# Transposing the attention output for the MLP: by DMA instead of TensorE and ScalarE

## The chip, the cores and the metric

The kernel runs on one core of a Trainium2 chip. The metric is the device time of one execution in microseconds. Engines are named as in the profile: PE (TensorE, with PEld for its weight loads), DVE (VectorE), ACT (ScalarE), POOL (GpSimd) and SP (SyncE, which here only issues DMAs).

## The reference

A linear attention (RWKV-5) over 4 batches, 8 heads, 768 tokens and a head dimension of 48, and then an MLP on its 3072 x 384 output. Cut to what is computed:

```python
state = np.zeros((B, H, D, D))
for t in range(S):
    cur = einsum('bhd,bhe->bhde', u[None] * k[:, :, t], v[:, :, t])
    y[:, :, t] = einsum('bhd,bhde->bhe', r[:, :, t], state + cur)
    state = w[None, :, :, None] * state + einsum('bhd,bhe->bhde', k[:, :, t], v[:, :, t])
x = y.transpose(0, 2, 1, 3).reshape(B * S, H * D)        # 3072 x 384
h = x @ w_in                                             # 384 x 2048
g = where(h >= 1, h, where(h <= -1, 0, (h + 1) ** 2 / 4))
out = g @ w_out                                          # 2048 x 384
```

## The kernel before

The tokens are cut into chunks of 128. A **unit** is one chunk of one batch (24 units), a **group** is the same chunk of two batches (12 groups of 2 units, 256 tokens). For each group the inputs R and K (float32, 384 KB each) are loaded by DMAs issued from SP (`load_rk`, lines 79 and 80), and V, cast to bf16, by DMAs from POOL (line 84). POOL also issues the loads of the MLP's weights: w_in in two halves before the loop, w_out in two halves at step 3. R and K have three buffers each.

One loop over steps `t` (line 379) carries all stages, each with its own offset; four steps belong to a group. All instructions are issued in the order in which the program writes them (`manual_schedule`), so each engine, SP among them, has one fixed queue. In a step the order is:

- `att0` on even steps (transposes of R and K on PE, copied to SBUF by DVE as TT), `att1` on odd steps (A on PE, masked by DVE into AT), from step 4g for group g
- at t = 4m, for m from 1: `load_rk` of group m + 2
- `act_end`: DVE forms `gt` from the square and h of the step before
- `mm1` (twelve matmuls `hp <- xT, w_in_sb`, line 310, four such parts to a group) and `act` (two ScalarE passes, lines 321 and 323). Group g begins `mm1` at t = 4g + 7
- `att2` on even steps (t = 4g + 2 and 4g + 4): the state update Sp, the attention output Y on PE, and DVE's sum `y` (line 271, bf16, two buffers); then `new_state`
- `att3` and `att4` on odd steps (t = 4g + 3 for the group's first unit, 4g + 5 for its second): the transposes of `y` (line 292) into the PSUM tile X, and the ScalarE copy (line 299) into one half of `xT[g]`. X takes the same PSUM buffer (tag `y`) as Y. Then `decay` on POOL
- `product` and `u_term`, the elementwise products, mostly on POOL, for groups ahead
- `mm2` (eight matmuls, line 341). On two steps of each group the result is copied by ScalarE (`o_sb`, line 347) and stored by a DMA from SP (line 349)

So `xT[g]` is what ties the attention to the MLP: both of its halves must be written before `mm1` of group g starts. The offset of the MLP is `L1`:

```python
L1, L2 = 7, 11
at_a, at_b, at_1, at_2, at_p = at(0), at(2), at(L1), at(L2), at(-4)
```

Before the loop, SP has issued R and K of groups 0, 1 and 2, and u.

Of the kernel before, what the change touches and what calls it, by code (L numbers as in the profile page):

```python
# [9 lines left out]
BF16 = mybir.dt.bfloat16  # L10
# [4 lines left out]
P = 128  # L15
# [3 lines left out]
UNITS = 2  # L19
# [3 lines left out]
def kernel(  # L23
# [11 lines left out]
    nc = tc.nc  # L35
# [6 lines left out]
    nK = DM // P  # L42
# [14 lines left out]
    ps1 = ctx.enter_context(tc.tile_pool(name="ps1", bufs=1, space=bass.MemoryType.PSUM))  # L57
# [8 lines left out]
    def load_tiles(g):  # L66
        R = loads.tile([P, UNITS * H, D], F32, name="R", tag="R")
        K = loads.tile([P, UNITS * H, D], F32, name="K", tag="K")
        V = loads.tile([P, UNITS * H, D], BF16, name="V", tag="V", bufs=5)
        loaded[g] = (R, K, V)  # L70
# [6 lines left out]
    def load_rk(g, j0=0, j1=UNITS):  # L77
        R, K, V = loaded[g]
        nc.sync.dma_start(out=R[:, j0 * H : j1 * H, :], in_=source(r, g, j0, j1))  # L79
        nc.sync.dma_start(out=K[:, j0 * H : j1 * H, :], in_=source(k, g, j0, j1))  # L80

    def load_v(g, j0=0, j1=UNITS):
        V = loaded[g][2]
        nc.gpsimd.dma_start(out=V[:, j0 * H : j1 * H, :], in_=source(v, g, j0, j1))  # L84
# [10 lines left out]
    def load_w_out(i):  # L95
        n = slice(i * nF // 2, (i + 1) * nF // 2)
        nc.gpsimd.dma_start(out=w_out_sb[:, n, :], in_=w_out_src[:, n, :])
# [20 lines left out]
    for j in range(UNITS):  # L118
# [13 lines left out]
    ident = const.tile([P, P], BF16, name="ident")  # L132
# [4 lines left out]
        out=umask, in_=umask, compare_op=ALU.is_ge, fill=1.0,  # L137
# [34 lines left out]
    def prepare_tiles(g):  # L172
        R, K, V = loaded.pop(g)
        KU = pre.tile([P, UNITS * H, D], F32, name="KU", tag="KU", bufs=2)
        RKU = pre.tile([P, UNITS * H, D], F32, name="RKU", tag="RKU")
        diag = pre.tile([P, UNITS * H], F32, name="diag", tag="diag")
        V2 = pre.tile([P, UNITS * H, D], F32, name="V2", tag="V2")
        ready[g] = (R, K, V, Rs[g % NB], Ks[g % NB], KU, RKU, diag, V2)

    def product(g, i, eng=None, j0=0, j1=UNITS):  # L180
        eng = eng or nc.gpsimd
        R, K, V, R_s, K_s, KU, RKU, diag, V2 = ready[g]

        def part(x):
            return x.rearrange("p (b h) d -> p b h d", b=UNITS)[:, j0:j1]

        def rep(x):
            return x.unsqueeze(1).to_broadcast([P, j1 - j0, H, D])

        if i == 0:  # L190
            eng.tensor_mul(part(R_s)[:, :, :, :D], part(R), rep(Wup))  # L191
        elif i == 1:
            eng.tensor_mul(part(K_s)[:, :, :, :D], part(K), rep(Wdn))  # L193
        elif i == 2:
            eng.tensor_mul(part(KU), part(K), rep(u_row))  # L195
        else:
            eng.tensor_mul(part(RKU), part(R), part(KU))  # L197

    def u_sums(g, j0=0, j1=UNITS):
        hs = slice(j0 * H, j1 * H)  # L200
        nc.vector.tensor_reduce(ready[g][7][:, hs], ready[g][6][:, hs, :], AX.X, ALU.add)  # L201

    def u_term(g, eng, j0=0, j1=UNITS):
        hs = slice(j0 * H, j1 * H)
        V, diag, V2 = ready[g][2], ready[g][7], ready[g][8]
        eng.tensor_mul(  # L206
            V2[:, hs, :], V[:, hs, :], diag[:, hs].unsqueeze(2).to_broadcast([P, (j1 - j0) * H, D])
        )


    unit = {}
    xT = {}

    def att0(n):
        g, j = divmod(n, UNITS)
        R_s, K_s = ready[g][3:5]
        T = ps1.tile([P, 2 * NP, P], BF16, name="T", tag="a")
        for i, x in enumerate((R_s, K_s)):
            for p in range(NP):
                h = j * H + 2 * p  # L220
                nc.tensor.transpose(T[:, i * NP + p, :], x[:, h : h + 2, :].rearrange("p h d -> p (h d)"), ident)  # L221
        TT = att.tile([P, 2 * NP, P], BF16, name="TT", tag="TT")
        nc.vector.tensor_copy(TT, T)  # L223
        unit[n] = [TT, None, None]

    def att1(n):
        TT = unit[n][0]
        A2 = [ps1.tile([P, NP, P], F32, name=f"A{j}", tag="ab"[j]) for j in range(2)]
        for p in range(NP):
            for j in range(2):  # L230
                rows = slice(j * HP, j * HP + D)
                nc.tensor.matmul(A2[j][:, p, :], TT[rows, NP + p, :], TT[rows, p, :], start=True, stop=True)  # L232
        AT = att.tile([P, 2, NP, P], BF16, name="AT", tag="AT")
        for j in range(2):
            nc.vector.tensor_mul(AT[:, j], A2[j], umask.unsqueeze(1).to_broadcast([P, NP, P]))  # L235
        unit[n][1] = AT
# [39 lines left out]
    def decay(n):  # L276
        g, j = divmod(n, UNITS)
        if n in decays:
            nc.gpsimd.tensor_mul(states[(g % BP) * UNITS + j], decays.pop(n), wCm)  # L279

    def new_state(n):
        g, j = divmod(n, UNITS)
        c, b = g // BP, (g % BP) * UNITS + j
        if c + 1 < NCH:
            nc.scalar.copy(states_bf[b], states[b])

    def att3(n):
        g, j = divmod(n, UNITS)
        y = unit.pop(n)[2]
        X = ps1.tile([P, nK, P], BF16, name="X", tag="y")  # L290
        for i in range(nK):
            nc.tensor.transpose(X[:, i, :], y[:, i * P : (i + 1) * P], ident)  # L292
        if j == 0:
            xT[g] = moe.tile([P, nK, TOK], BF16, name="xT", tag="xT", bufs=3)
        unit[n] = X

    def att4(n):
        g, j = divmod(n, UNITS)
        nc.scalar.copy(xT[g][:, :, j * P : (j + 1) * P], unit.pop(n))  # L299


    gs = {}
# [2 lines left out]
    def mm1(g, q):  # L305
        hp = psh.tile([P, FG, TOK], F32, name="hp", tag="h")
        for f in range(FG):
            n0 = (q * FG + f) * P
            for i in range(nK):
                nc.tensor.matmul(  # L310
                    hp[:, f, :], w_in_sb[:, i, n0 : n0 + P], xT[g][:, i, :], start=(i == 0), stop=(i == nK - 1),
                    skip_group_check=True,
                )
        h_ps[g, q] = hp
# [3 lines left out]
    def act(g, q):  # L318
        hp = h_ps[g, q]
        pt = moe.tile([P, FG, TOK], F32, name="pt", tag="pt")  # L320
        nc.scalar.activation(pt, hp, AF.Relu, bias=half_col, scale=0.5)  # L321
        sq = moe.tile([P, FG, TOK], F32, name="sq", tag="sq")
        nc.scalar.activation(sq, pt, AF.Square, bias=zero_col)  # L323
        sqs[g, q] = sq

    def act_end(g, q):
        hp, sq = h_ps.pop((g, q)), sqs.pop((g, q))
        gt = gpool.tile([P, FG, TOK], BF16, name="gt", tag="g")
        nc.vector.scalar_tensor_tensor(out=gt, in0=sq, scalar=1.0, in1=hp, op0=ALU.min, op1=ALU.max)  # L329
        gs[g, q] = gt  # L330
# [48 lines left out]
    for t in range(N):  # L379
        for n, odd in [(g * UNITS + i // 2, i % 2) for g, i in at_a.get(t, ())]:  # L380
            att1(n) if odd else att0(n)
            if n == 0:
                if odd:
                    u_sums(0, 0, 1)
                    u_term(0, nc.vector, 0, 1)
                else:
                    product(0, 0, nc.vector, 1, 2)
                    product(0, 1, nc.vector, 1, 2)
        if t % nQ == 0 and 3 <= t // nQ + 2 < nG:
            g = t // nQ + 2  # L390
            load_tiles(g)
            load_rk(g)
        if t % nQ == 1 and t // nQ + 2 < nG:
            load_v(t // nQ + 2)
        if t == 3:
            load_w_out(0)
            load_w_out(1)
        for g, q in at_e.get(t, ()):
            act_end(g, q)
        for g, q in at_1.get(t, ()):  # L400
            mm1(g, q)
            act(g, q)
        for n, odd in [(g * UNITS + i // 2, i % 2) for g, i in at_b.get(t, ())]:
            att3(n) if odd else att2(n)
            if odd:
                att4(n)
                decay(n)
            elif n:
                new_state(n - 1)
        if t == 2:  # L410
            u_sums(0, 1, 2)
            u_term(0, nc.vector, 1, 2)
        for g, i in at_p.get(t, ()):
            if g:
                if i == 0:
                    prepare_tiles(g)
                product(g, i)
        if t % nQ == 0 and 0 < t // nQ < nG:
            u_sums(t // nQ)
            u_term(t // nQ, nc.gpsimd)  # L420
        for g, i in at_2.get(t, ()):
            mm2(g, i)
# [30 lines left out]
```

## Time and profile before

| | |
|---|---|
| median of 3 runs | 203.04 us (202.64 to 203.18) |
| the profiled execution | 203.65 us, span 201.9 us |
| granted TensorE clock | 1.0 |
| PE busy | 171.6 us (85%) |
| PE weight loads | 129.3 us (64%) |
| ACT, DVE, POOL busy | 140.5, 140.3, 134.3 us |
| the transposes of y, line 292 | 72, 0.22 us each, overlapping one another |
| the copies into xT, line 299 | 24, 0.458 us each, 11.0 us of ACT |
| R and K loads in the steady part, from issue to landing | 4.4 and 6.0 us (median) |
| the output store, from issue to landing | 1.9 us (median) |

How to read what follows. Times run from the start of the span. A group row names line, engine, operation, what is written and read, the shape and the count; then busy time, mean ns of one, and the idle time just before, with what ended it. In the rows of slices each digit is the busy share, in tenths, of one fortieth of the span (5.05 us). The chain of waits is followed back from the last instruction, at each step to what released it. Queue q1 of the DMA rows is SP's, q0 is POOL's; their columns are packets, megabytes and the share of the 16 DMA engines' time. SPq is SP issuing a DMA.

### The profile page before, as it was taken

What the parts mean: (1) busy time and instruction counts of PE and PEld (TensorE: products, weight loads), DVE (VectorE), ACT (ScalarE), POOL (GpSimd) and SP (SyncE); (2) the same over time, 40 slices, a digit from 0 to 9 for tenths busy, and PEclk for the clock granted to TensorE, in tenths of its full rate; (3) what the DMA queues carried; (4) which work ended last, traced back from release to release, by engine and by line L of the source; (5) the groups of instructions that cost most, each with busy time, mean ns of one, the idle gap of its engine ahead of it and who ended that gap; (6) DMA issues with size and microseconds to landing.
All of it is one profiled execution on the core that took longest, in us unless ns stands there. A gap on an engine that the chain in (4) does not pass through costs nothing.

```text
span 201.9 us, 4347 instructions
## 1 busy us (share of the span) xinstructions
PE 171.6 (85%) x1768; PEld 129.3 (64%) x1768; DVE 140.3 (70%) x197; ACT 140.5 (70%) x173; POOL 134.3 (67%) x102
## 2 busy tenths in 40 slices
PE   0045419979999999999999999999999999999782
PEld 0023317767778777877787778777877786777541
DVE  3189636598968888869688888697787876543320
ACT  4511010789887878787878787878788878898810
POOL 7079999989798796996996969969969020000000
PEclk9999999999999999999999999999999999999999
DMA  5999999999978278836873785568110111101121
GB/s 110 171 212 187 202 135 172 182 158 174 173 45 177 63 64 171 77 82 128 67 152 85 42 196 65 76 136 81 39 40 4 39 42 39 42 0 41 39 78 42
DMA packets 81044, 20.34 MB, mean 101 GB/s; under 512 B 74880, under 2 KB 80256, under 8 KB 81024
## 3 DMA queue, kind: packets, MB, share of 16 engines
q1 hardware_dynamic: 53168, 14.36, 34.6%
q0 software_dynamic: 27712, 5.51, 31.4%
q8 instruction: 14, 0.23, 0.5%
q10 hardware_dynamic: 144, 0.20, 0.5%
q14 instruction: 6, 0.05, 0.1%
HBM read 20.84 MB, written 4.72 MB: 127 GB/s over the span
## 4 chain that ended last, share of the span: by engine, by line
PE 75%; POOL 8%; DVE 4%; DMA 3%; ACT 3%; issue 3%; SPq 2%; POOLq 0%; ACTq 0%
PE hp L310 31%; PE op L341 29%; PE T L221 5%; PE A L232 3%; DMA u_bc<-in_u_dram 3%; PE Y L259 2%; POOL KU L195 2%; PE X L292 2%; POOL RKU L197 2%; PE Y L254 2%; ACT pt L321 2%; SPq L79 2%; PE Sp L247 1%; ACT o_sb L347 1%; POOL V L84 1%
## 5 line engine op out<-in xcount | busy, mean ns | idle before, releaser
L321 ACT ACTIVATE pt<-hp,half_col 128x1024 f32<-128x1024 f32 x48 | 53.4, 1113 | 31.6 <-PE hp L310 31.3
L310 PE MATMUL hp<-xT,w_in_sb 128*128 128x256 bf16 x576 | 72.9, 278 | 1.1 <-DVE gt L329 1.1
L341 PE MATMUL op<-w_out_sb,gt 128*128 128x384 bf16 x384 | 69.9, 326 | 2.3 <-ACT o_sb L347 2.0
L329 DVE SCALAR_TENSOR_TENSOR gt<-sq,hp 128x1024 bf16<-128x1024 f32 x48 | 58.2, 1213 | 12.5 <-ACT sq L323 12.5
L310 PEld LDWEIGHTS <-w_in_sb 128*128 128x128 bf16 x576 | 54.8, 99 | 10.7 <-issue 1.4
L323 ACT ACTIVATE sq<-pt,zero_col 128x1024 f32<-128x1024 f32 x48 | 55.2, 1149 | 1.6
L341 PEld LDWEIGHTS <-gt 128*128 128x128 bf16 x384 | 35.2, 97 | 22.3 <-issue 3.1
L235 DVE TENSOR_TENSOR AT<-A,umask 128x512 bf16<-128x512 f32 x48 | 30.8, 683 | 7.4 <-PE A L232 7.2
L223 DVE COPY TT<-T 128x1024 bf16<-128x1024 bf16 x24 | 16.6, 690 | 21.8 <-PE T L221 21.8
L206 POOL TENSOR_TENSOR V<-V,diag 128x768 f32<-128x768 bf16 x11 | 16.2, 1474 | 20.6 <-DVE diag L201 20.3
L221 PE MATMUL T<-ident,Rs 128*128 128x128 bf16 x96 | 10.3, 237 | 18.7 <-DVE Rs L191 10.1
L195 POOL TENSOR_TENSOR KU<-K,u_bc 128x768 f32<-128x768 f32 (+1 forms) x13 | 22.0, 1689 | 6.4 <-DMA u_bc<-in_u_dram 6.4
L197 POOL TENSOR_TENSOR RKU<-R,KU 128x768 f32<-128x768 f32 (+1 forms) x13 | 22.1, 1700 | 0.3
L221 PEld LDWEIGHTS <-Rs 128*128 128x128 bf16 x96 | 8.0, 106 | 21.6 <-DVE Rs L191 10.6
L299 ACT COPY xT<-X 128x384 bf16<-128x384 bf16 x24 | 11.0, 460 | 14.3 <-PE X L292 14.3
L193 POOL TENSOR_TENSOR Ks<-K,Wdn 128x768 bf16<-128x768 f32 x11 | 20.0, 1817 | 0.0
L191 POOL TENSOR_TENSOR Rs<-R,Wup 128x768 bf16<-128x768 f32 x11 | 19.9, 1813 | 0.0
L279 POOL TENSOR_TENSOR state<-Tm,wCm 128x384 f32<-128x384 f32 x16 | 16.0, 1002 | 0.1
L347 ACT COPY o_sb<-op 128x384 f32<-128x384 f32 x24 | 11.2, 467 | 5.7 <-PE op L341 5.7
L232 PE MATMUL A<-TT 48*128 48x128 bf16 x192 | 11.6, 232 | 3.4 <-DVE TT L223 2.0
L84 POOL DMA_DIRECT2D V<-in_v_dram x12 | 14.4, 1202 | 0.0
L201 DVE TENSOR_REDUCE diag<-RKU 128x16 f32<-128x768 f32 (+1 forms) x13 | 11.5, 881 | 3.1 <-POOL RKU L197 3.1
(48 smaller groups left out, 145.8 us busy)
## 6 DMA issues: line engine op xcount, KB each, us to landing
out_dram<-o_sb SPq DMA_DIRECT2D x24, 192.0 KB, 1.9
R<-in_r_dram SPq DMA_DIRECT2D x11, 384.0 KB, 4.4
K<-in_k_dram SPq DMA_DIRECT2D x11, 384.0 KB, 6.0
V<-in_v_dram POOLq DMA_DIRECT2D x12, 192.0 KB, 5.0
w_in_sb<-in_moe_w_in_dram POOLq DMA_DIRECT2D x2, 768.0 KB, 9.0
w_out_sb<-in_moe_w_out_dram POOLq DMA_DIRECT2D x2, 768.0 KB, 17.1
R<-in_r_dram SPq DMA_DIRECT2D x2, 192.0 KB, 6.0
K<-in_k_dram SPq DMA_DIRECT2D x2, 192.0 KB, 5.4
```

The lines of the kernel that those rows point to most:

```text
L191: eng.tensor_mul(part(R_s)[:, :, :, :D], part(R), rep(Wup))
L193: eng.tensor_mul(part(K_s)[:, :, :, :D], part(K), rep(Wdn))
L195: eng.tensor_mul(part(KU), part(K), rep(u_row))
L197: eng.tensor_mul(part(RKU), part(R), part(KU))
L221: nc.tensor.transpose(T[:, i * NP + p, :], x[:, h : h + 2, :].rearrange("p h d -> p (h d)"), ident)
L232: nc.tensor.matmul(A2[j][:, p, :], TT[rows, NP + p, :], TT[rows, p, :], start=True, stop=True)
L235: nc.vector.tensor_mul(AT[:, j], A2[j], umask.unsqueeze(1).to_broadcast([P, NP, P]))
L310: nc.tensor.matmul(hp[:, f, :], w_in_sb[:, i, n0 : n0 + P], xT[g][:, i, :], start=(i == 0), stop=(i == nK - 1), skip_group_check=True,)
L321: nc.scalar.activation(pt, hp, AF.Relu, bias=half_col, scale=0.5)
L323: nc.scalar.activation(sq, pt, AF.Square, bias=zero_col)
L329: nc.vector.scalar_tensor_tensor(out=gt, in0=sq, scalar=1.0, in1=hp, op0=ALU.min, op1=ALU.max)
L341: nc.tensor.matmul(o_ps[g], gs[g, q][:, f, j * P : (j + 1) * P], w_out_sb[:, n, :], start=(n == 0), stop=(n == nF - 1),)
```

## The change

`att3` no longer transposes on PE, and `att4` is gone. Instead SP issues one transposing DMA per unit, from `y` in SBUF (128 tokens x 384, bf16) to that unit's half of `xT[g]` (three blocks of 128 x 128, bf16), at the same place in the program. Everything else stays in its place and order.

```diff
     def att3(n):
         g, j = divmod(n, UNITS)
         y = unit.pop(n)[2]
-        X = ps1.tile([P, nK, P], BF16, name="X", tag="y")
-        for i in range(nK):
-            nc.tensor.transpose(X[:, i, :], y[:, i * P : (i + 1) * P], ident)
         if j == 0:
             xT[g] = moe.tile([P, nK, TOK], BF16, name="xT", tag="xT", bufs=3)
-        unit[n] = X
-
-    def att4(n):
-        g, j = divmod(n, UNITS)
-        nc.scalar.copy(xT[g][:, :, j * P : (j + 1) * P], unit.pop(n))
+        nc.sync.dma_start_transpose(out=xT[g][:, :, j * P : (j + 1) * P], in_=y)
...
             att3(n) if odd else att2(n)
             if odd:
-                att4(n)
                 decay(n)
```

## Prediction

> **What bounds the kernel now.** I read the page first: the slices and the chain of waits say which engine the end hangs on, and when.
>
> ```profile
> PE   0045419979999999999999999999999999999782
> DMA  5999999999978278836873785568110111101121
> PE 75%; POOL 8%; DVE 4%; DMA 3%; ACT 3%; issue 3%; SPq 2%; POOLq 0%; ACTq 0%
> L299 ACT COPY xT<-X 128x384 bf16<-128x384 bf16 x24 | 11.0, 460 | 14.3 <-PE X L292 14.3
> ```
>
> A slice is 5.05 us. PE is nearly full from the seventh slice on (from 33 us) and carries 75% of the chain. The DMA engines are full from 5 us to about 52 us, and only there: the head is the stage in which a new transfer has to queue. The ScalarE copy that the change removes is not in the chain; its 14.3 us of idle time lie before 27 us.
>
> Next the chain in order of time, in the steady part (start, us, what):
>
> ```profile
> 93.90 1.42 PE hp L310 x12
> 95.31 0.17 PE X L292 x3
> 95.48 1.30 PE op L341 x8
> ...
> 100.71 1.42 PE hp L310 x12
> ```
>
> Two steps of the loop take 6.81 us of PE without a gap, and the three transposes of one unit are 0.17 us of it. The last line is the first matmul group of the next MLP group, at t = 4m+3 when these transposes are at t = 4m+1.
>
> Then the timeline of SP alone, because the new DMA is issued there (start, us taken; L79 is R, L80 is K):
>
> ```profile
> 12.74 1.49 SPq L80 DMA_DIRECT2D K<-in_k_dram  x1
> 16.59 1.97 SPq L79 DMA_DIRECT2D R<-in_r_dram  x1
> 18.66 9.11 SPq L80 DMA_DIRECT2D K<-in_k_dram  x1
> 28.67 5.18 SPq L79 DMA_DIRECT2D R<-in_r_dram  x1
> 33.94 9.40 SPq L80 DMA_DIRECT2D K<-in_k_dram  x1
> ```
>
> and the DMA view narrowed to the first three of these issues (the last number is us from issue to landing):
>
> ```profile
> K<-in_k_dram SPq DMA_DIRECT2D x1, 384.0 KB, 14.9
> ```
>
> ```profile
> R<-in_r_dram SPq DMA_DIRECT2D x1, 384.0 KB, 15.5
> ```
>
> ```profile
> K<-in_k_dram SPq DMA_DIRECT2D x1, 384.0 KB, 24.7
> ```
>
> I call the loads of group g Rg and Kg. K2 lands at 12.74 + 14.9 = 27.6 us, R3 at 16.59 + 15.5 = 32.1, K3 at 18.66 + 24.7 = 43.4. They land in the order of issue, and K3's issue holds SP until 27.77, just when K2 has landed; K4's holds it until 43.34, just when K3 has. So in the head SP's queue is a line in which each transfer waits for all before it. The reason is in the queues between 16 and 30 us:
>
> ```profile
> q0 software_dynamic: 3055, 1.78, 89.7%
> q1 hardware_dynamic: 3420, 0.65, 39.6%
> ```
>
> POOL's queue (w_in, w_out, V) takes over twice the engines' time that SP's gets. In steady state the same loads land in 4 to 6 us.
>
> Last, the timeline between 18 and 36 us, for what the first transposes have to meet:
>
> ```profile
> 25.06 0.55 DVE L271 TENSOR_TENSOR y<-Y,V 128x384 bf16<-128x384 f32 x1
> ...
> 33.05 2.74 PE L310 MATMUL hp<-xT,w_in_sb 128*128 128x256 bf16 x12
> ```
>
> y of unit 1 is there at 25.61; the first MLP matmul, which needs units 0 and 1, starts at 33.05.
>
> **Removed from PE.** 72 transposes. Units 0 and 1 (18.6 and 25.7 us) run while PE idles: nothing. Unit 2 (35.80) stands in the chain with 0.32 us. Unit 3 (41.5) lies where VectorE carries the chain: nothing. Units 4 to 23, at 47.63 and every two steps until 175.4, stand in full PE: 20 x 0.17 = 3.4 us. Together **-3.7 us**. From 178 us on PE and ScalarE alternate, and what arrives earlier there ends earlier.
>
> **Removed from ScalarE.** 24 x 0.458 = 11.0 us, none in the chain; I price it at nothing. The cover is PE: ScalarE has 2.97 us of work in a step of 3.4 us, before as in the steady part. The PSUM bank that X shared with Y also loses a reader; what ended PE's waits there was y, which stays.
>
> **Added in steady state.** A transposing DMA Dn per unit n on SP. For the odd unit of a group SP comes to it after the output store, issued at 94.86 and taking 0.36; y was ready at 93.21. So it is issued at 95.22 and its data are wanted at 100.71, or 0.17 sooner in the changed kernel: 5.3 us. No transposing DMA is in this trace. Below, the output store (half of SBUF's side of an R load, same queue, 128 partitions) lands in 1.9 us; above, a K load of four times the bytes lands in 5.5 (median, issue included). I take 2.5, nearer to the store, since 96 KB is less than either moves. Both ends fit in 5.3 us but for 0.2: no stall. The even unit has two more steps. Behind it on SP wait the next R and K, which are wanted over 13 us later, and the stores, which nobody waits for. By the page "VectorE: DVE Perf Modes" of the Trainium skill (section on the three transpose paths) TensorE is the better path wherever PSUM will do, at 390 ns for a 128x128 block against 1309 ns by DMA. The trace has 0.17 us for three blocks on a busy PE, less than that rule's figure; three blocks by its DMA figure would be an estimated 3.9 us, which still fits and would leave this term at nothing.
>
> **Added in the head.** SP issues in the order of the program: K2 before the loop, D0 at t = 3, R3 and K3 at t = 4, D1 at t = 5, D2 at t = 7, R4 and K4 at t = 8, D3 at t = 9. Follow it. D0 waits for y of unit 0 (18.50). R3 and K3, ready at 16.59, now wait behind it; R3 is first read by POOL at 38.8 and K3 at 43.9, so this alone costs nothing. D0 stands behind K2, lands after 27.6, and unit 0 is wanted at 33.05: nothing. y has two buffers, so y of unit 2 (32.40) must wait for D0 as well: some 3 us are left. **D1 is the one that matters.** SP can issue it only behind K3, and what stands before it in line is what K3 waits for in the trace, plus K3, plus D0. K3 lands at 43.4 there. D0 and D1 each add their own passage: 96 KB at the 174 GB/s of all queues between 16 and 30 us is 0.56 us, and at the pace that K3 got (384 KB in 43.4 - 32.1 = 11.3 us) a quarter of that, 2.8 us. I take 1.3 for each, nearer to the short end, since one wide transfer should be cut in fewer packets than K's. D1 lands at 43.4 + 1.3 + 1.3 = 46.0. PE, in order, stands at the first hp for 46.0 - 33.05 = **+12.95 us**, and with it ScalarE, VectorE behind gt, and POOL behind VectorE's sums.
>
> Is it made up later? From 33 to 46 us the chain runs through PE, ScalarE and VectorE in turn, and each is behind that same hp; from 46 on PE is full. So the whole delay goes to the end. D3 follows K4, now late itself but by then without the weights beside it (w_out has landed by 45.2); its y comes at 40.3 + 12.6 = 52.9 and it is wanted at 46.2 + 12.6 = 58.8: nothing.
>
> **The sum.** Profiled execution 203.65 us (span 201.9 and 1.75 around it): 203.65 + 12.95 - 3.7 = 212.9. That execution lies 0.6 above the median of the runs, 203.04; on the median +9.25 gives **212.3 us**. With D0 and D1 at 0.56 each it is 210.8, at 2.8 each 215.3. Two more unknowns widen it. While SP waits for D0 (16.59 to some 19.8) POOL's queue has the engines to itself and may be through sooner, which can bring K3 forward by at most these 3.2 us: 207.6. Or D0's issue holds SP until K2 has landed; then the line runs empty and R3 starts afresh, at most 3.9 us (an R load from issue to landing, at 61.26): 219.2.
>
> The page "DMA: Bandwidth & Descriptors" (section on queues, rings and completion order) has SP own one ring on each DMA engine, consumed in ring order, with no order of completion promised between transfers. It fits the landing times above, which were needed to show that the wait is this long; were a late transfer free to pass, the first rival below would hold.
>
> **The rivals.** (1) Faster: the transposes do not stand in the loads' line, by a ring of their own or by passing. SP is free of K3's issue at 27.8 us, D1 would land some 2.5 us later, at 30.3, before 33.05, and only the -3.7 remains: 199.3. For it: no run here shows which line a transposing DMA takes. Against it: all 26 loads, the u load and the 24 stores of SP share queue 1 in the page. It decides from D1 landing less than 3.7 us after 33.05, at 36.7. (2) Slower still: a transposing DMA takes over 5.3 us even in a free queue. At 7 us (a K load beside little else, at 7.63) each of the ten groups 2 to 11 adds 1.7 us, 17 in all, on top of the forecast: 229. For it: a transposed write is scattered; against it: every row with up to four times its bytes lands sooner in steady state. (3) The DMA does not transpose as one transfer but element by element: 49152 packets of 21 ns (queue 1's mean: 34.6% of 16 x 201.9 us over 53168) on 16 engines are 64 us a unit and over 1500 us in all. I give that next to nothing and count it under (2).
>
> **Chances.** Forecast 0.79, rival (1) 0.12, (2) and (3) 0.06; 0.03 for a head stall of about the size of the gain. The timed runs spread by 0.27%, so 0.3% (0.6 us) is about what can be told from no change: faster by more 0.12, within it 0.02, slower 0.86. The range is that of the forecast, 207.6 to 219.2; both rivals lie outside it and hold 0.18.
>
> **What would show it.** Right: in the changed profile hp's first matmul waits some 13 us, released by a DMA into xT; the DMA view has the second transposing DMA landing over 12 us after its issue; ScalarE's busy time is 11 us and PE's some 4 us lower in the middle; two steps take 6.64 instead of 6.81 us. Wrong: D1 landing before 36 us, waits on xT at the first hp of each MLP group in the middle, or steps that stay at 6.81.

## The result, and the profile after

| | before | after |
|---|---|---|
| median | 203.06 us | 213.46 us (213.3 to 214.65, 4 runs) |
| ratio | | 1.054 (1.050 to 1.058) |
| profiled execution, span | 203.65, 201.9 us | 214.65, 212.8 us |

The forecast was 212.3 us. The ratios in this document are taken over all runs on record (two more of the changed kernel, 213.69 and 214.8 us, beside the four of the table) but leave out runs over 1.5% above the fastest of their kernel, so that a ratio can differ from that of the medians beside it.

The page after, with the lines that answer to those shown of before (line numbers are the changed file's: hp is L303, op L334):

```profile
PE   0141422018699999999998999999999999999873
DMA  6999999998188879388796786767821211211111
PE 65%; DMA 13%; POOL 8%; ACT 4%; DVE 4%; issue 3%; SPq 2%; POOLq 0%; ACTq 0%; DVEq 0%
xT<-y SPq DMA_TRANSPOSE x24, 2.4
```

A slice is now 5.32 us. PE is nearly empty in the seventh to ninth slices (digits 2, 0 and 1), where it used to become full, and DMA, which had 3% of the chain, has 13%. The last row is the DMA list: in the median a transposing DMA lands 2.4 us after its issue. Where the chain stands in the steady part (start, us, what):

```profile
93.18 1.42 PE hp L303 x12
94.60 1.30 PE op L334 x8
...
99.83 1.42 PE hp L303 x12
```

Between hp and op the 0.17 us of transposes are gone, and two steps take 6.65 us instead of 6.81. The loss is all in the head. SP's own timeline there:

```profile
12.36 1.51 SPq L80 DMA_DIRECT2D K<-in_k_dram  x1
18.16 4.74 SPq L292 DMA_TRANSPOSE xT<-y  x1
23.00 0.55 SPq L79 DMA_DIRECT2D R<-in_r_dram  x1
23.60 6.90 SPq L80 DMA_DIRECT2D K<-in_k_dram  x1
30.59 9.81 SPq L292 DMA_TRANSPOSE xT<-y  x2
```

These are K2, D0, R3, K3, then D1 and D2. The DMA view, narrowed to the issue of one after another (us to landing last):

```profile
K<-in_k_dram SPq DMA_DIRECT2D x1, 384.0 KB, 15.6
...
xT<-y SPq DMA_TRANSPOSE x1, 12.6
...
R<-in_r_dram SPq DMA_DIRECT2D x1, 384.0 KB, 11.8
...
K<-in_k_dram SPq DMA_DIRECT2D x1, 384.0 KB, 21.6
...
xT<-y SPq DMA_TRANSPOSE x1, 16.1
```

With the issue times they land at 28.0, 30.8, 34.8, 45.2 and 46.7 us, in the order of issue. And the timeline at that moment, with the idle time and its releaser in brackets:

```profile
46.83 2.72 PE L303 MATMUL hp<-xT,w_in_sb 128*128 128x256 bf16 x12 [13.53 <-DMA xT<-y]
```

hp begins 46.83 - 33.05 = 13.8 us later. From there to the end of the span it is 165.97 us, against 168.85 before: 2.9 us are won back. 13.8 - 2.9 = 10.9 is the difference of the two spans.

### The profile page after: what moved, and what is told of

Read it like the earlier page. It is cut to its first block, busy times and chain, and to the rows that moved or that the text cites. A ratio compares the mean times of both kernels' runs of the same rounds, so it can differ in the third digit from the quotient of the medians.

```text
span 212.8 us, 4230 instructions
## 1 busy us (share of the span) xinstructions
PE 166.5 (78%) x1696; PEld 124.6 (59%) x1696; DVE 140.4 (66%) x197; ACT 131.7 (62%) x149; POOL 134.2 (63%) x102
## 3 DMA queue, kind: packets, MB, share of 16 engines
q0 software_dynamic: 27712, 5.51, 33.4%
## 4 chain that ended last, share of the span: by engine, by line
PE 65%; DMA 13%; POOL 8%; ACT 4%; DVE 4%; issue 3%; SPq 2%; POOLq 0%; ACTq 0%; DVEq 0%
PE hp L303 28%; PE op L334 27%; DMA xT<-y 10%; PE T L221 4%; PE A L232 3%; DMA u_bc<-in_u_dram 3%; ACT pt L314 2%; POOL KU L195 2%; POOL RKU L197 2%; PE Y L259 2%; PE Y L254 2%; SPq L79 1%; DVE gt L322 1%; PE Sp L247 1%; ACT o_sb L340 1%
## 5 line engine op out<-in xcount | busy, mean ns | idle before, releaser
L303 PE MATMUL hp<-xT,w_in_sb 128*128 128x256 bf16 x576 | 72.4, 276 | 15.3 <-DMA xT<-y 14.2
L334 PE MATMUL op<-w_out_sb,gt 128*128 128x384 bf16 x384 | 69.8, 325 | 2.3 <-ACT o_sb L340 2.0
L303 PEld LDWEIGHTS <-w_in_sb 128*128 128x128 bf16 x576 | 54.6, 99 | 24.7 <-issue 15.6
L334 PEld LDWEIGHTS <-gt 128*128 128x128 bf16 x384 | 36.0, 97 | 22.7 <-issue 3.1
L206 POOL TENSOR_TENSOR V<-V,diag 128x768 f32<-128x768 bf16 x11 | 16.2, 1475 | 32.7 <-DVE diag L201 31.1
L235 DVE TENSOR_TENSOR AT<-A,umask 128x512 bf16<-128x512 f32 x48 | 30.8, 682 | 7.3 <-PE A L232 7.3
L221 PEld LDWEIGHTS <-Rs 128*128 128x128 bf16 x96 | 7.9, 105 | 22.4 <-DVE Rs L191 10.2
L285 ACT CAST state_bf<-state 128x384 bf16<-128x384 f32 x20 | 9.9, 497 | 13.8 <-DVE state L269 13.8
L84 POOL DMA_DIRECT2D V<-in_v_dram x12 | 14.4, 1203 | 0.0
L271 DVE TENSOR_TENSOR y<-Y,V 128x384 bf16<-128x384 f32 x24 | 13.1, 548 | 0.5 <-POOL V L206 0.5
```

What stands on the lines that cost most here:

```text
L303: nc.tensor.matmul(hp[:, f, :], w_in_sb[:, i, n0 : n0 + P], xT[g][:, i, :], start=(i == 0), stop=(i == nK - 1), skip_group_check=True,)
L334: nc.tensor.matmul(o_ps[g], gs[g, q][:, f, j * P : (j + 1) * P], w_out_sb[:, n, :], start=(n == 0), stop=(n == nF - 1),)
```

## The experiments

My theory: the cost is one wait, that of D1 in SP's line behind K3, and every transposing DMA that finds its line empty is a gain. Rivals: a cost spread over all 24; the loads that the new DMAs push back; a transposing DMA that is slow by itself beside the weight loads.

### One transposing DMA alone

Kernel e1, `att3` as in the change for one unit and as before for the others:

```diff
+        if n == 1:
             nc.sync.dma_start_transpose(out=xT[g][:, :, j * P : (j + 1) * P], in_=y)
+        else:
+            # X, the three transposes and the ScalarE copy, as before the change
```

> Only unit 1 is transposed by DMA; the other 23 units as before the change. Line theory (the one transfer D1 waits on SP's queue behind K3): R3 goes out at 16.6 us again, K3 lands at some 43.4, D1 some 1.5 us after it (the distance in the changed kernel), so the first hp starts at about 45 instead of 33.05; none of the PE savings (unit 1's transposes ran while PE idled). Time 203.06 + 12 = 215. Rival, cost spread evenly over the 24 transposing DMAs (10.4 us / 24 = 0.43 each): 203.5.

Measured: 215.38 us, ratio 1.062 (1.060 to 1.063). Who waited for whom (us in total, times, longest):

```profile
PE hp L309 <- DMA xT<-y: 11.4, 1, 11.4
```

One transposing DMA of 24 makes the kernel slower than all 24 do, for the other 23 bring what is saved on PE. K3 was issued at 21.51 and landed 21.4 us later, at 42.9; D1 landed 28.03 + 16.5 = 44.5; hp began at 44.62. An even cost is out.

### The transposing DMAs with nobody waiting

Kernel e4, all 24 DMAs issued in their place, but into a tile of their own, while TensorE and ScalarE write xT:

```diff
-        y = att.tile([P, DM], BF16, name="y", tag="y")
+        y = att.tile([P, DM], BF16, name="y", tag="y", bufs=4)
...
-        nc.sync.dma_start_transpose(out=xT[g][:, :, j * P : (j + 1) * P], in_=y)
+        Z = moe.tile([P, nK, P], BF16, name="Z", tag="Z")
+        nc.sync.dma_start_transpose(out=Z, in_=y)
+        # X, the three transposes and the ScalarE copy, as before the change
```

> The transposes stay on TensorE with ScalarE's copy as before the change; the 24 transposing DMAs are issued as well, in the same place on SP, into a tile that nobody reads (y gets four buffers, so that y of units 2 and 3 need not wait for D0 and D1). So the line is as long as in the changed kernel, but no matmul waits for its end. Line theory: D1 still lands at some 46 us, and the time is that of before, 203.0 to 204.3 (up to 1.3 us if POOL gets K3 that much later). Rival, that the loads pushed back by the transposing DMAs cost the time: 10 us or more, 213.

Measured: 203.66 us, ratio 1.004 (1.002 to 1.005). The line is as long as ever; the DMA view at D1's issue (28.64 us) and the timeline of the first hp:

```profile
Z<-y SPq DMA_TRANSPOSE x1, 17.3
```

```profile
32.69 2.74 PE L309 MATMUL hp<-xT,w_in_sb 128*128 128x256 bf16 x12
```

D1 lands at 45.9 (46.7 in the change), and hp starts at 32.7 because it needs nothing of it. So all but 0.7 us of the cost is the wait, and neither the traffic nor the loads pushed back (R3 goes out at 22.4 here). The two extra buffers of y are not the difference either: in the changed kernel only hp waits for a transposing DMA (14.2 us in two waits), and the sum y waits for none. Where the remaining 0.7 us lie I did not trace.

### Why the line is slow

Kernel e6, w_out two steps later on POOL's queue:

```diff
-        if t == 3:
+        if t == 5:
             load_w_out(0)
             load_w_out(1)
```

> As the changed kernel, but w_out is loaded at t = 5 instead of t = 3, some 8 us later on POOL's queue. Line theory with the weight loads as the reason why the line is slow: K3 passes faster, D1 lands at 38 to 41 instead of 46.7, stall 5 to 8 instead of 13.5 us; w_out then lands near 50, about when it is wanted: 205 to 208. Rival, that the line is slow for SP's own packets and not for queue 0: D1 stays at 46 and the time at 213.

Measured: 208.28 us, ratio 1.024 (1.019 to 1.028). D1 is issued at 30.07 (30.59 in the changed kernel) and lands 8.7 us later, at 38.7 instead of 46.7. The two waits that are left:

```profile
PE hp L303 <- DMA xT<-y: 7.4, 2, 4.9
```

4.9 is D1; the other 2.5 is D3, which is now the one behind weights and loads. The forecast did not have it, and the time is 0.3 us above its range. D1's 8 us show that the load of w_out on POOL's queue makes up much of what slows SP's line; D1 still stands behind K3, and 8.7 us is not the 2.4 of an empty line.

### Moving the first unit that goes by DMA

Kernels e2 and e2b are e1's edit with `n >= 4` and `n >= 2` in place of `n == 1`.

> Units 0 and 1 as before the change, units 2 to 23 by DMA. Line theory: the stall comes back at the next group: D3 is behind R4 and K4, which land at 47.9 and 51.9 before, and unit 3 is wanted at 46.2; D3 at about 53.4, stall some 7 us, savings 3.7: 206.5. If D2's wait for y of unit 2 (33 us) holds R4 and K4 back by 4 us, up to 209. Rival, that the first transposing DMA alone is dear: it is now D2, with slack to 46 us, and the time is 199.5.

Measured: 210.97 us, ratio 1.039 (1.037 to 1.040). The wait comes back one group later, as the line theory says, but dearer than I had it. K4 landed at 53.8 instead of 51.9 and D3 at 55.0. The chain around it, and two stretches of the trace (length, busy time of each engine, granted clock as the third number from the end):

```profile
55.05 2.74 PE hp L309 x12
57.79 2.01 PE op L340 x8
...
60.25 1.31 PE hp L309 x12
```

```profile
45.00:56.00 11.00, 1.70 (x20) 1.10 (x17) 3.28 (x5) 2.37 (x3) 6.61 (x5) 0.68 1.52 123
56.00:60.00 4.00, 4.00 (x24) 2.50 (x23) 0.00 (x0) 2.14 (x2) 0.00 (x0) 0.61 0.79 132
```

The first hp of the group starts 8.8 us later than the 46.22 of before, and PE had lost its clock by then: the groups that take 1.42 and 1.30 us in the steady part take 2.74 and 2.01, another 2.0 us. 203.0 + 8.8 + 2.0 - 3.4 = 210.4. The Trainium skill, page "TensorE: Matmul & The Clock Gate", section on the clock gate, puts the fall to half the clock at an idle window of about 3.4 us; here an idle time of 9.2 us has done it, with the granted clock at 0.68 and 0.61 where the stretches beside it have 1.00. Less was enough elsewhere: in the profiled executions of e2 and e8 a wait of 3.0 us was followed by a granted clock of 0.50, while in e6 the wait of 2.5 us for D3 left it at 1.00.

> Units 0 to 3 as before the change, units 4 to 23 by DMA. Line theory: D4 is the first; from 54 us on SP's loads land in 4 to 6 us, D5 follows K5 (landing at 55.7 before) and is wanted at 59.8, so no stall; 20 x 0.17 us of PE saved: 203.06 - 3.4 = 199.7. Rival, even cost: 20/24 of the loss, 211.7.

Measured: median 202.11 us, and the four runs lie far apart (200.09, 200.91, 203.3 and 204.81). The ratio, 0.988 (0.985 to 0.990), rests on the lower two, some 200.5 us: the sign is as forecast, the gain 0.8 us short. In the profiled execution, of 204.81 us, K5 landed at 57.6, not 55.7, and D5 at 62.6; hp waited 3.0 us for it, and PE ran without its full clock after it. I take it that in some runs the wait is short enough to escape the second cost; that was not traced.

### Putting the loads behind

Kernel e3, the change with R and K of group m+2 issued after `att3` of step 4m+1:

```diff
         if t % nQ == 0 and 3 <= t // nQ + 2 < nG:
             g = t // nQ + 2
             load_tiles(g)
-            load_rk(g)
...
             att3(n) if odd else att2(n)
...
+        if t % nQ == 1 and 3 <= t // nQ + 2 < nG:
+            load_rk(t // nQ + 2)
```

> As the changed kernel, but R and K of group m+2 are issued at the end of step 4m+1 instead of the start of step 4m, so behind the odd unit's transposing DMA: D1 ahead of R3 and K3, D3 ahead of R4 and K4. Line theory: D1 has only K2 (27.6) and D0 ahead, lands near 31 to 32.5, and the first hp starts at 33 to 33.5; R3 and K3 come later, so D3 may land at 46 to 49 with unit 3 wanted at 46.2: a stall of 0 to 3 us, and POOL may wait some us for R4. Time 203.06 - 3.7 + 0 to 4: 199.5 to 203.5, 201 the likeliest. Rival, that a transposing DMA beside the weight loads is slow by itself: D1 still lands 13 to 16 us after its issue, some 213.

Measured: 205.49 us, ratio 1.010 (1.006 to 1.015): the order of the line is worth 8 us, and still it is 1% slower than before, above the forecast of 199.5 to 203.5. D1 did what was forecast (issued at 25.92, landed at 33.4, hp at 33.5). What came after it I had too small (read from the profiled execution, of 208.02 us, the longest of the four):

```profile
45.11 1.82 POOL L191 TENSOR_TENSOR Rs<-R,Wup 128x768 bf16<-128x768 f32 x1 [6.16 <-DMA R<-in_r_dram]
...
49.84 0.56 DVE L271 TENSOR_TENSOR y<-Y,V 128x384 bf16<-128x384 f32 x1 [3.60 <-DMA xT<-y]
...
50.25 2.74 PE L303 MATMUL hp<-xT,w_in_sb 128*128 128x256 bf16 x12 [3.57 <-DMA xT<-y]
```

R3 now comes 6.2 us too late for POOL, D2 still holds one of y's two buffers, and hp waits 3.6 us for D3, and at half speed (2.74 us). The line was only cut at one place.

### Another queue

Kernel e5, the change with `nc.scalar.dma_start_transpose`, so that the transposes have ScalarE's queue to themselves.

> As the changed kernel, but the transposing DMAs are issued from ScalarE, whose DMA queue carries only one other transfer. Line theory: D1 is issued at some 25.3 us and has no load ahead of it; it shares the DMA engines with the other two queues and lands by 31; no stall in the head, 3.7 us saved: 199.4. Against it stands the issue itself: if the 1.18 us that SP needs for one are taken from ScalarE too, two steps hold 4.5 + 0.5 + 0.5 + 1.2 = 6.7 us of it against 6.64 of TensorE, and the odd unit's DMA goes out behind two activations, at about 97.6 on the clock of before, 2.4 us before landing and 3.1 before it is wanted: up to 203. Rival, that a transposing DMA beside the weight loads is slow by itself: D1 13 us or more, 213.

Measured: 211.72 us, ratio 1.041 (1.034 to 1.047). That is far over the forecast of 199.4 to 203. The first hp is nearly as forecast: D1 is issued at 26.24, lands 6.8 us later (by 33.0, not 31), hp waits 0.5 us for it and starts at 33.1. So even with no load ahead a transposing DMA takes 6.8 us beside the weights, but not 16. In all hp waited for a DMA nine times, 10.0 us. The longest wait is still in the head, 4.2 us for D3, which was issued at 43.39 and landed 7.0 us later, and again at half speed:

```profile
50.45 2.74 PE L303 MATMUL hp<-xT,w_in_sb 128*128 128x256 bf16 x12 [4.19 <-DMA xT<-y]
```

The other seven waits, 5.3 us together, lie in the steady part, one in each of seven groups. One of them in the timeline:

```profile
90.20 1.20 POOL L84 DMA_DIRECT2D V<-in_v_dram  x1
...
91.20 1.20 ACTq L292 DMA_TRANSPOSE xT<-y  x1
...
96.66 1.49 PE L303 MATMUL hp<-xT,w_in_sb 128*128 128x256 bf16 x12 [1.47 <-DMA xT<-y]
```

ScalarE comes to the issue behind two activations, and now V's load is 1 us ahead. This DMA landed 5.4 us after its issue; in the changed kernel, issued 0.24 us before V's, one lands in 2.6. I had counted the late issue, not the neighbour that it runs into.

### A version that beats both

The odd unit's slack can be had in another way: issue the DMA on the even step, right behind y, ahead of the output store. Kernels e8 (from unit 4) and e10 (from unit 6) do so, beside e1's edit with `n >= 4` and `n >= 6`; e9 is from unit 6 with the issue where the change has it.

```diff
+            if not odd:
+                att2(n)
+            if odd == (n < 6):       # e8: n < 4
+                att3(n)
-            att3(n) if odd else att2(n)
```

> Units 0 to 3 as before the change; from unit 4 on by DMA, issued on the even step right behind y's sum, so ahead of the output store instead of behind it: 1.9 us more slack for the odd unit. Theory (the remaining stalls of the variant from unit 4 are late landings against 5.3 us of slack): no wait of hp on a DMA, 20 x 0.17 us saved, 199.7 in every run. Rival, that a transposing DMA costs something beside its wait: 200.5 or more, as the variant from unit 4.

Measured: median 200.28 us, ratio 0.985 (0.982 to 0.989), runs from 199.31 to 206.07. Not "199.7 in every run". In the profiled execution, of 206.07 us, D5 is still in line behind K5: K5 landed at 58.0 and D5 at 62.6; hp waited 3.0 us for it and then ran at half speed. Why D5 took another 4.6 us after K5 was not tested; a load of V on POOL's queue (issued at 54.69) ran beside it.

> Units 0 to 5 as before the change, units 6 to 23 by DMA, issued behind the output store as in the change. Theory: the 3.0 us that hp still waited in the variant from unit 4 were D5 behind R5 and K5, which D4's own wait had pushed back; from unit 6 on every odd transposing DMA finds an empty line. Saving 18 x 0.17 = 3.1 us: 200.0, with up to 1 us more in a run in which one lands over 5.3 us after its issue. Rival, that the transposing DMAs cost something beside their waits (0.66 us for 24 unread ones): 200.5.

Measured: 200.72 us (200.38 to 201.1), ratio 0.989 (0.987 to 0.991). The wide spread is gone, but 0.7 us of the saving are missing. One odd DMA in the profiled execution, issued at 81.11, landed 5.5 us later, and hp waited 0.3 us; the rest I could not place.

> As the variant from unit 6, but issued on the even step right behind y's sum, ahead of the output store: 1.9 us more slack for the odd unit. Theory: no wait of hp on a DMA anywhere, 200.0 in every run, the most even of all variants. Rival, that slack is not what varies from run to run: the same time and the same spread as the variant that issues behind the store.

Measured: **200.05 us** (199.91 to 200.4), ratio 0.986 (0.984 to 0.987), with no wait of hp on a DMA in the trace. The saving is 2.95 us, against 18 x 0.17 = 3.06. So 18 DMAs without a late one show no cost beside the waits that could be measured, and the earlier issue brings back what e9 was short of. This median is the lowest of all and the runs lie closest together; by the ratio, which leaves out its run of 206.07 us, e8 is as fast.

## Why the prediction was right

The time was 1.2 us above the forecast and inside its range; the changed kernel's profiled execution lies 1.2 us over its own median, so spans compare with a little more than medians (10.9 and 10.4 us).

- **The stall of D1**, forecast 12.95 us, was 13.8 by the start of hp. D1 behind K3 in SP's line is shown by e1 (alone, it brings the loss), by e4 (landing nearly as late with no one waiting, it costs 0.7 us) and by e3 and e5 (without K3 ahead, hp starts at 33.5 and 33.1).
- **Its terms.** D0's passage was 30.8 - 28.0 = 2.8 us, where I took 1.3: the long end of the range, a quarter of K3's time for a quarter of its bytes. So the reason for the short end, that one wide transfer is cut in fewer packets, did not carry. D1's was 1.5 against 1.3, and K2 landed 0.4 us later. K3 came 14.4 us behind what stood before R3 (15.8 in the trace of before), which gave 1.4 of that back. That D0's error and K3's nearly cancel is luck.
- **The saving on PE**, forecast 3.7 us: 168.85 - 165.97 = 2.9, and a second wait for a transposing DMA (14.2 us in two waits, less the 13.5, so 0.7, at 113 us) hides the rest: some 3.6. The steps went to 6.65 us, forecast 6.64.
- **The steady part**: landing 2.4 us, forecast 2.5, and no stall but that one, in which a DMA landed 5.8 us after its issue against 5.3 of slack. (Of the full R and K loads before the change, those issued from 58 us on land in 4.1 and 5.1 us; the medians 4.4 and 6.0 in the table ahead of the prediction take in the head.) D3 is moved by 12.6 us in the prediction where its own sum has 12.95; D3 fits with either: it was issued at 54.09, landed at 56.4 and was read at 59.9.
- **ScalarE**: busy time fell by 8.8 us, not by the 11 that the prediction named as a sign: some of the copies overlapped their neighbours in the record (the groups of ScalarE add up to some 6 us more than its busy time before, to some 4 after). It was off the chain as assumed.
- **That nothing is made up later** held: the first hp ran at the slow pace (2.72 us) as before (2.74), and PE was full afterwards.
- **The two unknowns** that widened the range were not needed to hold the result. SP was indeed held by D0 (4.74 us), but R3 was issued at 23.0, well before D0 landed at 30.8, and the line did not run empty. Whether the 1.4 us by which K3 came sooner are the other unknown, POOL's queue being through earlier, was not separated.

## What to carry to other kernels

Before a DMA is put on an engine's queue, find its place in that queue's line: read the landing times of the transfers issued just before it, in the stage where it will stand, and not its own duration. A step of 0.17 us on a full engine is worth moving to a DMA only where the line is empty and the slack holds the late landing, not the median one; keep the old way for the few units of the head. When such a DMA is wanted by a full engine, issue it right behind its producer, ahead of stores that wait for something else.

## What the runs showed that I had not expected

- A wait in a kernel that is already running fast can cost more than its length. After the waits for D3 (9.2 us in e2b, 4.2 in e5, 3.6 in e3) hp's next group took 2.74 us instead of 1.42. After the 2.5 us in e6 it did not (1.47). In the change itself nothing was added, because the first hp is slow both before (2.74) and after (2.72).
- A transposing DMA of 96 KB holds SP for 1.18 us and lands in 2.3 to 2.6 us in an empty line, where an output store takes 1.9. But single ones come late: in the change and in e9 one landed 5.8 and 5.5 us after its issue, and both times the trace has a 16 KB packet of queue q8 (instructions) starting 0.55 to 0.58 us after the issue and lasting 1.9 and 1.5 us. That packet alone does not make up the delay: in e9 another one started 0.59 us after the issue at 128.02, with no load of V beside it, and that DMA landed 3.6 us after its issue. I did not test that this is the cause.

```profile
107.88 5.82 DMA xT<-y
113.74 1.47 PE hp L303 x12
```

The chain of the changed kernel shows the late one: between two hp groups stands a DMA, where before there are only steps of PE.
